# Moving an expert block's transposes into another block's second layer, in a fused attention, MLP and mixture-of-experts kernel

## The chip, the cores and the metric

The kernel runs on one core of one Trainium2 chip. The metric is the device time of one execution in microseconds (us). The engines are named as the profile names them: PE is TensorE (PEld its weight loads), DVE is VectorE, ACT is ScalarE, POOL is GpSimd, SP is SyncE.

## The reference, cut to what matters

Three stages follow each other: attention in chunks of 32 positions, an MLP with a sigmoid gate over the 1536 tokens of 512 numbers that come out of it, and a mixture of 8 experts in which each token goes to the one expert with the largest logit. The change touches the third stage:

```python
logits = x @ w_gate                       # 1536 x 8
expert_idx = np.argmax(logits, axis=1)
gate_w = softmax(logits)[arange(N), expert_idx]
# disp[e]: the tokens of expert e in order, at most cap = 384 of them
h = np.maximum(np.einsum('ecd,edf->ecf', disp, w1), 0.0)   # d = 512, f = 1024
y = np.einsum('ecf,efd->ecd', h, w2)
out[i] = gate_w[i] * y[expert_idx[i], pos[i]]              # for each kept token i
```

## The kernel before

**Precision.** Each product of two float32 matrices is made as three TensorE products: both operands are split into a high part and the rest, and high times high, high times rest and rest times high are summed in PSUM. The expert weights are split on the core: a piece is 128 x 1024 numbers (512 KB), loaded by SyncE's queue into one of eight "raw" tiles (L239), the high part is made on ScalarE (L293) and the rest on VectorE (L298). An expert has eight pieces, four for w1 and four for w2. The split pieces lie in six slots of two pieces. The pieces of an expert are made while the one before it is computed: `w_next(e, keep)` converts the next piece unless `keep` pieces of expert e+1 are done, and a slot must be free. `KEEPS` gives the three bounds of `keep`: after the first layer of an expert, after the second layer of its first block, and in the last part. Inside the first layer, `PUMPS` and `PUMPS1` say behind which group of matmuls a piece is converted.

**Experts and blocks.** The tokens of an expert are handled in blocks of up to 128: first, second and third. The experts are worked in the order `EORDER`; below, "expert 0" is the first of that order. The number of tokens is only known on the chip, so the engines branch on counts read into registers (`tc.If`, `both`): an expert with one block runs `first_of`, one with two `first_of_two` (both blocks in one first layer, 256 columns, L862). Then `thirds_first` branches on a third block: `small_h` where it has at most 64 rows ("narrow": high part and rest lie side by side in one operand), `wide_h` where it has more, `skip` where there is none: one tiny matmul (L1001). After it the two slots of w1 are free. `after_arms` makes the gate and the second layer of the first block (L985), `second` or `second_not` and `rest` the other blocks; a narrow block's output is made by `small2` (L922, then L925 to L928). The If arms are scheduled as a unit; the instructions around them are placed by a list scheduler, which may draw an independent instruction ahead of a branch, and `in_order` keeps a stretch of code in the order written.

**Rows of the tokens.** A block's tokens are gathered from a table in memory by an indirect DMA on GpSimd's queue (L812) into a tile "xr" of a pool with six of them in rotation, transposed on TensorE (L829), and copied by ScalarE (L833) and VectorE (L834) into the split operand "xs". `next_trans` makes the transposes of the next expert's two blocks behind the first layer of an expert (in `first_of`: ahead of the last four transposes, `turn`, of its hidden layer, L954). The finished rows are scattered into the output by an indirect DMA on the same queue (L995, L928).

**The first block.** The first block of expert 0 is computed ahead of the branches, between the steps of the routing of the last tokens (`first_block`): a generator of 50 steps, nearly each one matmul, drawn by `go`. Its second layer (L767) ends the stage. Then the counts are read, expert 0's second block is gathered and transposed (`parts[0].load(1)`, `parts[0].trans(1)`), an arm for fewer than 128 tokens is branched over (L1109), and `first_of(1)` makes that block's first layer (L945).

## Time and profile before

| what | us |
|---|---|
| median of 3 runs | 534.36 |
| lowest, highest run | 533.71, 535.32 |
| the profiled execution, its own time | 533.77 |
| its span, from the first instruction to the last | 531.9 |
| attention, MLP and routing, up to the first matmul of expert 0's second block | 352.5 |
| from there to the end of the span | 179.4 |

The mean TensorE clock that the chip granted was 0.992 of full speed. The page of the profile gives busy times and shares of the span by engine; the views used below list waits by engine and line, instructions in order of time, the chain of work that ended last, and DMA issues with their time to landing. Lines as L945 are lines of the kernel before.

### The profile page before, as it was taken

To read this page: it belongs to the slowest core of one execution; us is meant where nothing else is said; L and a number is where in the kernel's file an instruction comes from. 1 tells how busy PE (TensorE), PEld (TensorE's weight loads), DVE (VectorE), ACT (ScalarE), POOL (GpSimd) and SP (SyncE) were. 2 spreads that over 40 slices of the span, in tenths; PEclk is the share of its full clock that TensorE was granted. 3 is DMA by queue.
4 is the path that set the end of the run, shared out by engine and by line. 5 is a ranking of instruction groups with operands and counts; after the bars stand their busy time and mean duration, and the time that the engine had idled before them with its cause. 6 is when DMAs were issued, how large, how long until landed. Compare 5 with 4: busy or idle time off the path is not lost. (4 is left out here: it accounts for less than half of the span.)

```text
span 531.9 us, 10859 instructions
## 1 busy us (share of the span) xinstructions
PE 509.4 (96%) x4192; PEld 438.5 (82%) x4192; DVE 312.1 (59%) x609; ACT 275.2 (52%) x553; POOL 117.1 (22%) x114
## 2 busy tenths in 40 slices
PE   8799999999999999999999999989999898899994
PEld 3589888898998899989988888768888786789893
DVE  4999894588892282322256444738446757756631
ACT  2798986856752352222255334547355665654521
POOL 3244442332410031000000000252113322311121
PEclk9899999999999999999999999999999999999997
DMA  8888555041440004000059301599536868855010
GB/s 306 277 327 307 199 188 172 1 160 63 171 148 15 0 2 159 0 1 1 10 168 286 110 36 49 168 319 351 195 116 222 282 234 257 290 215 173 23 29 29
DMA packets 38913, 80.62 MB, mean 152 GB/s; under 512 B 3897, under 2 KB 10041, under 8 KB 38842
## 3 DMA queue, kind: packets, MB, share of 16 engines
q1 hardware_dynamic: 36010, 70.66, 39.2%
q0 software_dynamic: 2832, 9.01, 5.2%
q8 instruction: 45, 0.74, 0.6%
q14 instruction: 26, 0.21, 0.1%
HBM read 70.16 MB, written 9.75 MB: 150 GB/s over the span
## 5 line engine op out<-in xcount | busy, mean ns | idle before, releaser
L545 PEld LDWEIGHTS psh<-xT,w 128*128 128x128 f32 x1152 | 147.0, 188 | 8.3 <-DVE xT L518 0.4
L588 PE MATMUL acc<-w,g 128*128 128x512 f32 x576 | 153.0, 400 | 0.0
L545 PE MATMUL psh<-xT,w 128*128 128x256 f32 x1152 | 151.9, 281 | 0.1
L588 PEld LDWEIGHTS acc<-w,g 128*128 128x128 f32 x576 | 100.6, 188 | 19.5 <-issue 2.1
L560 ACT ACTIVATE sg<-psh 128x256 f32<-128x256 f32 x96 | 36.8, 384 | 126.0 <-PE psh L545 124.3
L298 DVE TENSOR_TENSOR w<-raw,w 128x1024 fp32r<-128x1024 f32 x64 | 76.4, 1222 | 30.2 <-ACT w L293 26.6
L568 DVE TENSOR_TENSOR g<-sg,g 128x256 fp32r<-128x256 f32 x78 | 38.2, 490 | 80.3 <-ACT g L564 77.7
L293 ACT ACTIVATE w<-raw 128x1024 fp32r<-128x1024 f32 x64 | 65.4, 1054 | 13.1 <-PE psy L1001 10.0
L862 PE MATMUL psh<-xs,w 128*128 128x256 f32 x480 | 59.2, 283 | 3.8 <-DVE hT L866 3.8
L862 PEld LDWEIGHTS psh<-xs,w 128*128 128x128 f32 x480 | 57.9, 188 | 4.4 <-DVE hT L866 4.2
L985 PE MATMUL psy<-w,hT 128*128 128x512 f32 x240 | 59.8, 401 | 0.0
L985 PEld LDWEIGHTS psy<-w,hT 128*128 128x128 f32 x240 | 44.0, 188 | 9.7
L812 POOL DMA_INDIRECT xr<-rows,taker x21 | 30.1, 1432 | 33.2 <-DVE small L791 15.9
L564 ACT ACTIVATE g<-psh 128x256 fp32r<-128x256 f32 x96 | 36.4, 380 | 0.0
L599 DVE SCALAR_TENSOR_TENSOR x<-acc,x 128x512 f32<-128x512 f32 x36 | 24.1, 686 | 20.1 <-PE acc L588 20.1
L721 POOL DMA_INDIRECT y<-rows,taker x1 | 1.2, 1224 | 123.8 <-DVE cnt_i L728 123.8
L865 ACT ACTIVATE hT<-psh 128x256 fp32r<-128x256 f32 x40 | 14.5, 380 | 25.8 <-PE psh L862 25.8
L866 DVE SCALAR_TENSOR_TENSOR hT<-psh,hT 128x256 fp32r<-128x256 f32 x40 | 16.1, 421 | 19.2 <-ACT hT L865 19.0
L298 POOL TENSOR_TENSOR w<-w,w 128x512 fp32r<-128x512 f32 x12 | 16.7, 1400 | 41.6 <-ACT w L293 41.6
L263 ACT ACTIVATE w<-raw 128x512 f32<-128x512 f32 x32 | 21.3, 676 | 8.4 <-DMA raw<-in_w_out_dram 6.8
L288 POOL TENSOR_TENSOR w<-w,rest 128x512 int32<-128x512 int32 x13 | 17.4, 1340 | 36.8 <-DVE w L274 33.8
L274 DVE SCALAR_TENSOR_TENSOR w<-raw,w 128x512 int32<-128x512 int32 x32 | 24.7, 780 | 0.3
(153 smaller groups left out, 568.0 us busy)
## 6 DMA issues: line engine op xcount, KB each, us to landing
raw<-in_w_dram SPq DMA_DIRECT2D x64, 512.0 KB, 5.7
raw<-in_w_out_dram SPq DMA_DIRECT2D x16, 512.0 KB, 4.4
raw<-in_w_in_dram SPq DMA_DIRECT2D x16, 512.0 KB, 3.7
vt<-in_v_dram SPq DMA_DIRECT2D x12, 512.0 KB, 5.3
kt<-in_k_dram SPq DMA_DIRECT2D x12, 368.0 KB, 5.4
qt<-in_q_dram SPq DMA_DIRECT2D x12, 256.0 KB, 5.0
out_dram<-blank SPq DMA_DIRECT2D x12, 256.0 KB, 2.7
rows<-x SPq DMA_DIRECT2D x5, 520.0 KB, 4.8
```

Source lines behind the costliest of these rows:

```text
L274: nc.vector.scalar_tensor_tensor(out=self.w, in0=self.words()[1], scalar=-0x40000000, in1=self.w, op0=ALU.bitwise_and, op1=ALU.bitwise_or)
L293: nc.scalar.activation(out=w_dst(self.name, self.i, 0), in_=w, func=AF.Copy)
L298: eng.tensor_tensor(out=lo, in0=w, in1=hi.bitcast(F32), op=ALU.subtract)
L545: nc.tensor.matmul(ps, lhsT=w[:, wz, c, i * P:(i + 1) * P], rhs=xT[tb][:, xz, c, :], start=n == 0, stop=n == 3 * KC - 1)
L560: nc.scalar.activation(out=sg_t[u], in_=h_t[u], func=AF.Silu, scale=1.702)
L564: g_last[:1] = [nc.scalar.activation(out=g[:, 0], in_=h_t.pop(u), func=AF.Silu, scale=1.702).ins]
L568: lo = eng.tensor_tensor(out=g[:, 1], in0=sg_t.pop(u), in1=g[:, 0].bitcast(F32), op=ALU.subtract)
L588: nc.tensor.matmul(acc_t[tb][s], lhsT=g[:, gz, s * P:(s + 1) * P], rhs=w[:, wz, wi, :], start=i == 0 and n == 0, stop=u == last_of(k, tb) ...
L599: nc.vector.scalar_tensor_tensor(out=dst, in0=acc_t[tb][s], scalar=1 / 1.702, in1=dst, op0=ALU.mult, op1=ALU.add)
L812: return nc.gpsimd.indirect_dma_start(out=t, out_offset=None, in_=rows[:, :], in_offset=bass.IndirectOffsetOnAxis(ap=taker[:, b, ex:ex + 1 ...
L862: mm = nc.tensor.matmul(ps, lhsT=w[:, wz, c, f0:f0 + P], rhs=t[:, xz, c, :], start=m == 0, stop=m == 3 * KC - 1)
L985: nc.tensor.matmul(ps, lhsT=h[:, hz, fc, o:o + P], rhs=w[:, wz, fc % 4, :], start=fc == 0 and n == 0, stop=fc == F2 - 1 and n == 2)
```

## The change

Five things change together.

1. **The second block of expert 0** is gathered (`load1`) before the rest of the first block's steps, and transposed eight steps before their end (`TAIL1`), into the tile that held the first block's operand, which is not read any more then. `adopt` hands that tile to the expert. The arm that is branched over takes its PSUM tiles from the pool "t" in place of "h".
2. **Room in SBUF:** the operand's tile moves to another pool; the gathered blocks have five tiles "xr" in place of six, and one "xrt" for third blocks in place of two.
3. **The first two chunks of the second layer** (`HEAD2`, six matmuls) move into the arms of the third block (`start2`): behind the transposes where there is one, in place of the tiny matmul where there is none.
4. **Weight pieces** are dealt 3, 4, 1 over the three parts of an expert in place of 3, 2, 3 (`KEEPS`), and the first pump of `first_of` is left out (`PUMPS1`).
5. **Narrow outputs** are scaled by the gate on VectorE, in the two operations that bring the halves together, in place of a third operation on ScalarE.

```diff
--- before.py
+++ after.py
@@ -39,14 +39,16 @@
 AHEAD = 4
 EARLY = 12
 KEEP = 4
-KEEPS = (3, 5, 8)
+KEEPS = (3, 7, 8)
 HALF = P // 2
-PUMPS1 = (1, 1, 1, 0)
+HEAD2 = 2
+PUMPS1 = (0, 1, 1, 0)
 GFC = 2
 EORDER = (1, 2, 0, 3, 4, 5, 6, 7)
 KNOWN = 8
 TFC = 5
 STEPS = (2, 4, 2, 5, 4)
+TAIL1 = 8
 DEPTH = 2
 STOP = False
 U1 = 74
@@ -613,7 +615,9 @@
             nc.tensor.transpose(ps[:, c * P:(c + 1) * P], x2[:, gi, c * P:(c + 1) * P], ident)
         s = gi - gs[0]
         if s == 0:
-            x2T_t[gi] = pool.tile([P, KC, len(gs) * P], F32, tag=f"x2T{len(gs)}", name="x2T", bufs=SUB + 1 - len(gs))
+            width = ROW if len(gs) == 1 else DM * len(gs)
+            t = pool.tile([P, width], F32, tag=f"x2T{len(gs)}", name="x2T", bufs=SUB + 1 - len(gs))
+            x2T_t[gi] = t[:, :DM * len(gs)].rearrange("p (c n) -> p c n", c=KC)
         nc.scalar.activation(out=x2T_t[gs[0]][:, :, s * P:(s + 1) * P], in_=ps.rearrange("p (c n) -> p c n", n=P),
                              func=AF.Copy)
 
@@ -710,7 +714,7 @@
         def load():
 
             f = first_block
-            f.xs = late_t["pool1"].tile([P, 2, KC, P], F32R, name="xs0")
+            f.xs = late_t["xs"]
             f.h = late_t["pool1"].tile([P, 2, F2, P], F32R, name="hT0")
             f.xr = late_t["y0"]
             nc.vector.tensor_scalar(out=taker0, in0=tk_t[0][:, EORDER[0]:EORDER[0] + 1], scalar1=float(NT), scalar2=None,
@@ -727,11 +731,19 @@
             nc.tensor.matmul(ps[:, :E], lhsT=ones, rhs=ohacc[:, 0], start=True, stop=True)
             nc.vector.tensor_copy(cnt_i[:, E:], ps[0:1, EORDER[0]:EORDER[0] + 1])
 
-        def trans():
+        def load1():
+            late_t["x1"] = late_t["pool"].tile([P, ROW], F32, tag="x2T1", name="x1", bufs=SUB)
+            return nc.gpsimd.indirect_dma_start(
+                out=late_t["x1"], out_offset=None, in_=rows[:, :],
+                in_offset=bass.IndirectOffsetOnAxis(ap=taker[:, 1, EORDER[0]:EORDER[0] + 1], axis=0),
+                bounds_check=NT, oob_is_err=False).ins
+
+        def trans(xr=None):
             f = first_block
             ps = psum("misc", "pst0")
+            xr = f.xr if xr is None else xr
             for c in range(KC):
-                nc.tensor.transpose(ps[:, c * P:(c + 1) * P], f.xr[:, c * P:(c + 1) * P], ident)
+                nc.tensor.transpose(ps[:, c * P:(c + 1) * P], xr[:, c * P:(c + 1) * P], ident)
             pv = ps.rearrange("p (c n) -> p c n", n=P)
             nc.scalar.activation(out=f.xs[:, 0], in_=pv, func=AF.Copy)
             nc.vector.tensor_tensor(out=f.xs[:, 1], in0=pv, in1=f.xs[:, 0].bitcast(F32), op=ALU.subtract)
@@ -741,7 +753,7 @@
             f = first_block
             order = [(xz, wz, c) for xz, wz in ((0, 0), (0, 1), (1, 0)) for c in range(KC)]
             p1 = [psum("lg", "psh0"), psum("acc0", "psh1")]
-            t = late_t["pool"].tile([P, KC, SUB * P], F32, tag=f"x2T{SUB}", name="hs0", bufs=1).rearrange("p c n -> p (c n)")
+            t = late_t["pool"].tile([P, SUB * DM], F32, tag=f"x2T{SUB}", name="hs0", bufs=1)
             f.hs = [t[:, 512 * j:512 * j + 512] for j in range(2)]
 
             def first(j, i):
@@ -804,10 +816,13 @@
     def expert_parts(e, ep, tp, cnt):
 
         ex = EORDER[e]
-        xr, xs, gt, hT = {}, {}, {}, {}
+        xr, xs, gt, hT, own = {}, {}, {}, {}, {}
+
+        def adopt(b, x):
+            own[b] = x
 
         def load(b):
-            t = ep.tile([P, ROW], F32, tag="xr" if b < 2 else "xrt", name="xr", bufs=6 if b < 2 else 2)
+            t = ep.tile([P, ROW], F32, tag="xr" if b < 2 else "xrt", name="xr", bufs=5 if b < 2 else 1)
             xr[b] = t
             return nc.gpsimd.indirect_dma_start(
                 out=t, out_offset=None, in_=rows[:, :],
@@ -816,6 +831,8 @@
 
         def xs_of(b):
 
+            if b in own:
+                return own[b], 0
             i = min(b, 2)
             key = 0 if i < 2 else b
             if key not in xs:
@@ -870,7 +887,7 @@
         def block(b):
 
             with in_order():
-                block_h(b)()
+                block_h(b, kind="t")()
                 layer2_part(b, y_of(b), range(F2))
             send(b)
 
@@ -890,6 +907,7 @@
                 pv = ps[:, :KC * HALF].rearrange("p (c n) -> p c n", n=HALF)
                 nc.scalar.activation(out=x[:, :, 0], in_=pv, func=AF.Copy)
                 nc.vector.tensor_tensor(out=x[:, :, 1], in0=pv, in1=x[:, :, 0].bitcast(F32), op=ALU.subtract)
+                start2()
                 hs = []
                 for j in range(2):
                     w_tile(("w1", e, j), 0)
@@ -922,14 +940,13 @@
                     nc.tensor.matmul(ps, lhsT=h[:, fc].rearrange("p z n -> p (z n)"), rhs=w[:, wz, fc % 4, :],
                                      start=fc == 0 and wz == 0, stop=fc == F2 - 1 and wz == 1)
             y = ep.tile([P, DM], F32, tag="y", name="y", bufs=2)[:HALF]
-            nc.vector.tensor_copy(y, ps[HALF:])
-            nc.vector.tensor_tensor(out=y, in0=ps[:HALF], in1=y, op=ALU.add)
-            nc.scalar.activation(out=y, in_=y, func=AF.Copy, scale=gt[b][:HALF])
+            nc.vector.tensor_scalar(out=y, in0=ps[HALF:], scalar1=gt[b][:HALF], scalar2=None, op0=ALU.mult)
+            nc.vector.scalar_tensor_tensor(out=y, in0=ps[:HALF], scalar=gt[b][:HALF], in1=y, op0=ALU.mult, op1=ALU.add)
             nc.gpsimd.indirect_dma_start(
                 out=out[:, :], out_offset=bass.IndirectOffsetOnAxis(ap=taker[:HALF, b, ex:ex + 1], axis=0),
                 in_=y, in_offset=None, bounds_check=NT - 1, oob_is_err=False)
 
-        def block_h(b, pump=lambda i: None):
+        def block_h(b, pump=lambda i: None, kind="h"):
 
             x, o = xs_of(b)
             h = hT_of(b)
@@ -939,7 +956,7 @@
                 w_tile(("w1", e, j), 0)
                 w = w_tile(("w1", e, j), 1)
                 if j not in p1:
-                    p1[j] = psum("h", "psh")
+                    p1[j] = psum(kind, "psh")
                 for xz, wz in ((0, 0), (0, 1), (1, 0)):
                     for c in cs:
                         nc.tensor.matmul(p1[j], lhsT=x[:, xz, c, o:o + P], rhs=w[:, wz, c, :],
@@ -949,7 +966,7 @@
                     nc.scalar.activation(out=hs[j], in_=p1[j], func=AF.Relu)
 
             def turn(j):
-                ps = psum("h", "psu")
+                ps = psum(kind, "psu")
                 for c in range(KC):
                     nc.tensor.transpose(ps[:, c * P:(c + 1) * P], hs[j][:, c * P:(c + 1) * P], ident)
                 n0 = b * P if b < 2 else 0
@@ -986,7 +1003,7 @@
                                      start=fc == 0 and n == 0, stop=fc == F2 - 1 and n == 2)
 
         def layer2(b):
-            layer2_part(b, y_of(b), range(F2))
+            layer2_part(b, y_of(b), range(HEAD2 if b == (1 if e == 0 else 0) else 0, F2))
             send(b)
 
         def send(b):
@@ -1054,10 +1071,18 @@
 
         def wide_h(b):
             trans(b)
+            start2()
             block_h(b)()
 
+        def start2():
+
+            b = 1 if e == 0 else 0
+            layer2_part(b, y_of(b), range(HEAD2))
+
         def thirds_first():
 
+            y_of(1 if e == 0 else 0)
+            assert NCB == 3
             for b in range(2, NCB):
                 hT_of(b)
                 xs_of(b)
@@ -1065,8 +1090,7 @@
                 def first():
                     both(cnt[ex] > b * P + HALF, lambda: wide_h(b), lambda: small_h(b))
 
-                y_of(1)
-                both(cnt[ex] > b * P, first, lambda: skip(1))
+                both(cnt[ex] > b * P, first, start2)
             for j in range(F // 512):
                 w_free(("w1", e, j))
 
@@ -1131,7 +1155,7 @@
             y_of(1)
             both(cnt[ex] > P, second, second_not)
 
-        return SimpleNamespace(load=load, trans=trans, xs_of=xs_of, after_first=after_first, others=others,
+        return SimpleNamespace(adopt=adopt, load=load, trans=trans, xs_of=xs_of, after_first=after_first, others=others,
                                before_arms=before_arms)
 
 
@@ -1176,6 +1200,7 @@
             wp2 = ctx.enter_context(tc.tile_pool(name="wp2", bufs=1, side="left"))
             free_slots.append(wp2.tile([P, 2, 2048], F32R, name="w4"))
             late_t["y0"] = wp2.tile([P, ROW], F32, name="y0")
+            late_t["xs"] = wp2.tile([P, 2, KC, P], F32R, name="xs0")
             late_t["known"] = wp2.tile([P, NCB * E], F32, name="known")
             plg = st.enter_context(tc.tile_pool(name="ps_lg", bufs=1, space=PSUM))
             ps_pools["lg"] = (plg, "lg", [P, 512])
@@ -1317,6 +1342,9 @@
             first_block.gate()
             while (("w2", 0, 1), 1) not in ready:
                 w_pump()
+            not_before.append(first_block.load1())
+            go(33 - TAIL1)
+            first_block.trans(late_t["x1"])
             go()
             first_block.finish()
     rt.close()
@@ -1337,13 +1365,11 @@
         free_slots.append(wp3.tile([P, 2, 2048], F32R, name="w5"))
         late_raw(RAWS)
         parts = [expert_parts(e, ep, tp, cnt) for e in range(E)]
-        not_before.append(parts[0].load(1))
-        with ExitStack() as behind:
-            for i in parts[0].trans(1):
-                behind.enter_context(tc.issue_after(i))
-            w_loads(8)
-            while w_next(-1):
-                pass
+        parts[0].load(1)
+        parts[0].adopt(1, late_t["xs"])
+        w_loads(8)
+        while w_next(-1):
+            pass
         w_end[0] = len(pieces)
         with tc.high_priority(offset=LOADS):
             w_loads(8 * (F // 512))
```

## Rows read from the trace of the kernel before

**Rows 1.** The page, busy time and share of the span by engine.
```profile
PE 509.4 (96%) x4192; PEld 438.5 (82%) x4192; DVE 312.1 (59%) x609; ACT 275.2 (52%) x553; POOL 117.1 (22%) x114
```

**Rows 2.** TensorE's waits from 350 us: waiter, releaser, total us, times, longest.
```profile
PE psh L862 <- DVE hT L866: 3.8, 2, 1.9
PE psu L954 <- ACT hs L949: 1.9, 1, 1.9
PE psh L945 <- ACTq L1109: 1.7, 1, 1.7
PE psh L900 <- DVE xs L892: 1.0, 1, 1.0
```

**Rows 3.** Timeline of the last narrow output: start, us, instruction, idle time before it.
```profile
524.49 0.69 DVE L925 COPY y<-psy 64x512 f32<-64x512 f32 x1 [2.49 <-DMA out_dram<-y,taker]
525.22 0.68 DVE L926 TENSOR_TENSOR y<-psy,y 64x512 f32<-64x512 f32 x1
525.98 0.72 ACT L927 ACTIVATE y<-y,gt 64x512 f32<-64x512 f32 x1 [4.37 <-issue]
```

**Rows 4.** TensorE's timeline, from the first block to expert 0's second.
```profile
350.11 0.60 PE L829 MATMUL pst<-ident,xr 128*128 128x128 f32 x4
...
352.52 4.48 PE L945 MATMUL psh<-w,xs 128*128 128x512 f32 x18 [1.71 <-ACTq L1109]
```

**Rows 5.** TensorE's timeline at expert 1's third block.
```profile
378.51 4.22 PE L985 MATMUL psy<-w,hT 128*128 128x512 f32 x17
382.66 0.46 PE L889 MATMUL pst<-ident,xr 64*128 64x64 f32 x4
384.10 4.00 PE L900 MATMUL psh<-w,xs 128*128 128x512 f32 x16 [0.98 <-DVE xs L892]
```

**Rows 6.** Tile xs, 340 to 390 us: ns min/median/max, first and last start.
```profile
L833 ACT ACTIVATE xs<-pst x5: 588/592/603, 350.9 to 378.8; 128x512 fp32r<-128x512 f32 x5
```

**Rows 7.** VectorE's timeline at expert 1's third block.
```profile
378.98 1.29 DVE L834 TENSOR_TENSOR xs<-pst,xs 128x512 fp32r<-128x512 f32 x2 [0.23 <-ACT xs L833]
...
380.61 1.23 DVE L298 TENSOR_TENSOR w<-raw,w 128x1024 fp32r<-128x1024 f32 x1
383.62 0.42 DVE L892 TENSOR_TENSOR xs<-pst,xs 128x256 fp32r<-128x256 f32 x1 [1.79 <-ACT xs L891]
```

**Rows 8.** GpSimd's timeline from 340 us, its gathers and scatters.
```profile
342.76 1.83 POOL L812 DMA_INDIRECT xr<-rows,taker  x1 [15.94 <-DVE small L791]
...
379.90 1.02 POOL L812 DMA_INDIRECT xr<-rows,taker  x1 [0.36 <-ACT ex L839]
...
404.06 0.93 POOL L928 DMA_INDIRECT out_dram<-y,taker  x1 [4.76 <-DMA out_dram<-y,taker]
405.30 1.16 POOL L812 DMA_INDIRECT xr<-rows,taker  x1 [0.30 <-POOLq L1047]
```

**Rows 9.** DMA issues from 404 to 407 us: median us from issue to landing.
```profile
xr<-rows,taker POOLq DMA_INDIRECT x1, 4.9
```

**Rows 10.** The chain that ended last, in expert 2: start, us, what.
```profile
407.05 0.87 PE pst L829 x8
...
412.46 0.11 PE psy L1001
```

**Rows 11.** Timelines of ScalarE, VectorE and TensorE between experts 4 and 5.
```profile
452.69 1.06 ACT L293 ACTIVATE w<-raw 128x1024 fp32r<-128x1024 f32 x1 [2.25 <-PE psy L1001]
...
453.78 1.22 DVE L298 TENSOR_TENSOR w<-raw,w 128x1024 fp32r<-128x1024 f32 x1 [1.65 <-ACT w L293]
456.30 5.77 DVE L298 TENSOR_TENSOR w<-raw,w 128x1024 fp32r<-128x1024 f32 x5 [1.29 <-PE psh L862]
...
454.53 6.01 PE L862 MATMUL psh<-xs,w 128*128 128x256 f32 x48
```

**Rows 12.** ScalarE's timeline at the start of expert 4.
```profile
442.85 0.72 ACT L927 ACTIVATE y<-y,gt 64x512 f32<-64x512 f32 x1 [3.86 <-issue]
...
444.42 0.58 ACT L949 ACTIVATE hs<-psh 128x512 f32<-128x512 f32 x1
```

**Rows 13.** The branches of one line on TensorE: ns min/median/max, first and last start.
```profile
L1047 PEldq COMPARE_BRANCH  x45: 65/184/3665, 359.6 to 520.0; - x45
```

## The prediction

> **What bounds the kernel now.** I read the page first: TensorE is busy 96% of the span, VectorE 59%, ScalarE 52% [rows 1]. So TensorE's order of work sets the end, and an edit counts only if it takes work off TensorE, fills one of its holes, opens a new one, or shortens what comes after its last matmul. The view of who waited for whom, cut to TensorE in the expert phase (from 350 us), names the holes [rows 2]: two of 1.9 us in the first layer of the two-block experts (L862 behind VectorE's L866), one of 1.9 us in L954 behind ScalarE's L949, one of 1.7 us where the first expert's second block starts (L945, behind ScalarE's queue at the branch L1109), one of 1.0 us in the narrow third block (L900). Together 8.4 us. The reader is to see that all five are waits for ScalarE or VectorE, none for weights from memory. Behind the last matmul follow a copy, an addition and a scaling before the last rows go out [rows 3].
>
> The arms taken can be read from the timeline: in the order of work, experts 0 to 7, only expert 1 has a third block (narrow), experts 2 and 4 have one block, 3, 6 and 7 a narrow second one.
>
> **Part 1, the early transposes.** Before, the four transposes L829 run when the first block is done, and the next matmul starts at 352.52 after 1.71 us of idling [rows 4]. The wait is put down to ScalarE reaching the branch L1109: the untaken arm shares the PSUM tiles "h" with L945. The change moves the arm to the tiles "t" and makes the transposes eight steps before the end. A step is 0.24 us (17 matmuls L985 start 4.15 us before the next group, [rows 5]), so eight cover 1.95 us; copy and subtraction take 0.59 us and 0.65 us [rows 6, 7], 1.3 us with the handoffs. The gather that feeds them is issued where the first one is now, at 342.76 [rows 8], more than 5 us ahead of them, and another gather follows it on GpSimd's queue, which shifts those behind it by 1.3 us. The weight loads on SP's queue are held for this gather as they now are for the first, so they start as before. TensorE does the same work; the hole goes: -1.7 us. Bounds: 0 (the start still waits for something ScalarE does at the branch) and -1.7. I take the full gain, since both causes that I can see are removed. If the cover were gone, it would cost 1.3 us.
>
> **Part 2, buffers.** To make room, the gathered blocks "xr" get five tiles in place of six, in rotation. Asked for in program order they are: expert 0's second block (#0), expert 1's two (#1, #2), expert 0's first, in the untaken arm (#3), expert 2's (#4, #5), expert 3's (#6, #7), and so on. With six, #7 reuses #1 and #8 reuses #2. The trace agrees: one gather is issued at 379.90, behind expert 1's first gate (L839), the next at 405.30, behind that expert's second arm and its last scatter at 404.06, which itself waits for the scatter before it [rows 8]. With five, #6 reuses #1 (so 379.90) and **#7, expert 3's second block, reuses #2**, so it goes to 405.30. It lands 4.9 us later [rows 9], at 410.2. But expert 2 has one block and is short: it makes expert 3's transposes from 407.05 on, eight in 0.87 us [rows 10], the second four at 407.5. So TensorE would stand for 2.7 us, in a place where it never waits now. All that stands in the order behind them (L954, the second layer) waits too. Bounds: 0 and 4. The other reuses fall at least 10 us ahead of need; the third blocks' single tile is released before its gather's turn on the queue. Cost: +2.7 us.
>
> **Part 3, two chunks of the second layer into the arms.** Six matmuls of the second layer stand in for the dummy L1001 in the arms not taken: seven dummies of 0.11 us go [rows 10], -0.8 us. The scheduler has so far pulled 17 matmuls of the second layer ahead of the third-block branch [rows 5]; they accumulate in one PSUM bank, so now none can pass the six. Where the arm is empty, TensorE does them later at no loss. Where it is taken (expert 1) it loses cover: from the start of the 17 to L900 were 5.59 us [rows 5]. Now VectorE has L834 twice to 380.27, a weight piece from 380.61 to 381.84, and L892 of 0.42 us [rows 7], so L900 can start at 382.30, 3.79 us after the same point; 11 matmuls fewer (2.68 us) lie in it, so idling grows by 2.68 - 1.80 = 0.9 us. Bounds: -0.7 (piece not ahead of it) and +0.9. I take +0.9: the piece is ahead today.
>
> **Part 4, pieces 3, 4, 1, the first pump gone, scaling on VectorE.** Weight pieces from the fifth on need a slot that comes free when TensorE has passed the third-block arm: today ScalarE idles 2.25 us for L1001 (expert 4) and VectorE 1.65 us, and then five pieces in one row (5.77 us) keep VectorE from L866, with the first layer's 48 matmuls of 6.01 us done and waiting [rows 11]. With the 17 matmuls behind the arm, the slot comes about 2.7 us sooner, and three pieces run under the second layer, not one. Work it out from the end of the twelve matmuls that make hs, in expert 4: VectorE's line is hs and one piece on ScalarE (0.58 + 1.06), ten pieces of 1.15, four subtractions of 0.65 to 0.7, gate 0.3, L866 0.4: 16.6 us; TensorE until it needs the bank back: 36 matmuls of 0.24, 16 transposes of 0.11, dummy 0.1, 48 of 0.122: 16.4 us. 0.2 us is left of the hole of 1.9. I take -1.6 us, as that assumes VectorE never idles (bounds 0 and -1.9). The same hole after expert 2 goes for certain if part 2 holds TensorE up by 2.7 us there: -1.9.
>
> The hole at L954: L949 starts at 444.42, because L927 of the narrow output before it sits in ScalarE's queue until 442.85, and the pump's piece follows [rows 12]. Both leave the queue, and L949 then waits for its own twelve matmuls alone, with six more queued ahead of L954 (1.4 us, against 0.58 for L949); -1.9 us, bounds 0 and -1.9. Behind L927 now nothing is queued on ScalarE; VectorE's two operations stay two, each with a PSUM operand as before, so 0.7 us each by [rows 3].
>
> At the end, the scaling of 0.72 us and its handoff of 0.08 go [rows 3]: -0.8 us.
>
> **Sum**, against the profiled execution's own 533.77 us (span 531.95 and 1.8 around it; 0.6 us under the median of the runs): -1.7 + 2.7 - 0.8 + 0.9 - 1.6 - 1.9 - 1.9 - 0.8 = -5.1, so **528.6 us**.
>
> **Rivals.**
> (a) *The gather is in time.* If the tiles aren't reused as I count, or the landing is hidden, the 2.7 us don't come, and the hole after expert 2 shrinks like the other (-1.6, not -1.9): 533.8 - 7.5 = 526.2 us. For it: I have the rotation only from the order of issues. Against: the two issues behind expert 1's gates fit it.
> (b) *The transition gains nothing.* L945 also depends on what ScalarE does last in the first block, or on the branch through another tile: 528.6 + 1.7 = 530.3 us.
> (c) *Slower: code behind the branch.* TensorE's branches take 0.18 us in the median, but up to 3.67 us [rows 13]. Today 17 matmuls (4.1 us) stand queued ahead of the third-block branch and hide that; afterwards eight transposes of 0.87 us, so a long one would show 2.8 us. Three of the seven arms where it struck would give 528.6 + 8.4 = 537 us, and it takes three for a slower kernel. Against: today's long branches lie at the narrow second arms, and TensorE's queue is already past the branch 2 us before the matmuls end. The Trainium skill ("Runtime: NRT & Kernel Launch", section Instruction fetch mechanics) says that a taken branch to a target outside the loaded pages forces a fetch by DMA before the engine goes on, and the duplicated matmuls make the arms longer; by that rule each such jump costs, while by the row most of 45 cost nothing to be seen.
>
> **How the numbers follow.** My forecast 0.57, (a) 0.20, (b) 0.14, (c) 0.06, something unseen 0.03. A difference of 0.3% (1.6 us) is about what a measurement of this kernel can tell. The range takes in (a) less 0.4 and the forecast with (b), and the bounds of part 2 (4 us of standing) with no gain at the first layer: 525.8 to 531.8 us. Faster by over 0.3% needs all the gains of 3.5 us to survive: the forecast, (a) and most of (b), 0.85. Within 0.3%: a part of (b) with the bounds against it, 0.08; slower: (c) and half of the unseen, 0.07.
>
> **What would show it.** Part 1: L945 follows L1001 of the transition at once. Part 2: TensorE waits in L829 for a gather by L812 in expert 2, some 2.7 us, and that gather is issued just behind a scatter L928 or its line afterwards. Part 3: seven fewer L1001; the wait of L900's line grows to nearly 2 us. Part 4: no wait of L954's line for L949, and less than 1 us of L862's for L866. End: no ScalarE instruction between the narrow output's two on VectorE and the last scatter. The forecast is wrong if TensorE waits behind the arms' branches, or not at all in expert 2.

## The result, and the profile after

The changed kernel takes 526.5 us (median of four runs, 525.63 to 527.21), the kernel before 534.84 in the runs made beside it: ratio 0.9846, 95% interval 0.9821 to 0.9872, so 1.3% to 1.8% faster. The prediction was 528.6, from 525.8 to 531.8; the time that came is near that of its rival (a), 526.2. The profiled execution of the changed kernel has 525.63 us of its own and a span of 523.8, which is 8.1 us less than before.

The five holes of [rows 2] first. TensorE's waits in the same stretch of the changed kernel (waiter, releaser, total us, times, longest):

```profile
PE pst L906 <- DVE xs L851: 1.2, 1, 1.2
PE psh L962 <- ACT y L806: 0.8, 1, 0.8
PE psy L1002 <- ACT xs L850: 0.7, 1, 0.7
PE psh L962 <- issue: 0.6, 1, 0.6
PE psh L918 <- DVE xs L909: 0.3, 1, 0.3
PE psh L879 <- DVE hT L883: 0.2, 1, 0.2
```

The lines have moved: the first layer L862 is L879 here, the second L985 is L1002, the block's first layer L945 is L962, the turn L954 is L971, the dummy L1001 is L1018, the narrow block's L889 and L900 are L906 and L918. Of 8.4 us in the large holes 3.8 us are left. The two behind the first layer and the one at the turn are gone but for 0.2; the one where the first expert's second block starts is half its size and has another releaser; the narrow third block's has grown from 1.0 to 1.2 + 0.3 (L906 and L918); and two are new, 0.7 ahead of L1002 and 0.6 ahead of L962.

Where the time came from shows when the expert phase is cut where each expert's first layer starts, from the end of the first block on. TensorE's windows of the kernel before (window, its length, busy time and matmuls, granted clock, DMA share, GB/s; experts 0, 1, 3, 4 and 5, and what follows the last matmul):

```profile
350.71:366.19 15.48, 13.77 (x68) 1.00 1.03 364
366.19:400.85 34.66, 33.68 (x206) 1.00 0.60 196
...
414.44:438.74 24.30, 22.39 (x146) 1.00 0.76 260
438.74:454.53 15.79, 13.85 (x68) 1.00 0.80 251
454.53:480.90 26.37, 24.45 (x155) 1.00 0.74 255
...
524.40:531.90 7.50, 0.00 (x0) 0.63 0.08 17
```

And of the changed kernel:

```profile
349.48:364.22 14.74, 13.91 (x68) 1.00 1.03 377
364.22:399.49 35.27, 33.82 (x205) 1.00 0.63 221
...
412.90:435.82 22.92, 22.10 (x145) 1.00 0.93 316
435.82:449.40 13.58, 13.54 (x65) 1.00 0.69 240
449.40:474.31 24.91, 24.10 (x155) 1.00 0.95 321
...
516.92:523.80 6.88, 0.00 (x0) 0.67 0.09 19
```

Stage by stage the difference is -0.74, +0.61, -0.18, -1.38, -2.21, -1.46, -0.49, -0.40 and -0.62: -6.87 us in all, with the granted clock at 1.00 in all eight expert stages of both. The other 1.2 us of the 8.1 lie ahead of the first stage: its start moved from 350.71 to 349.48, with expert 0's four early transposes ahead of it in both. That point falls between 348.3 and 351.9 in the profiled executions of all kernels of this study, so 1.2 us there can't be told from scatter. Experiments are therefore read below by the time from this point to the end of the span: 181.2 before, 174.3 after.

**Where there is no wait.** The prediction's dearest term was a stand of 2.7 us in expert 2, for expert 3's second gather. TensorE's timeline there, in the changed kernel (start, us, instruction; idle time before it in brackets):

```profile
405.51 1.04 PE L846 MATMUL pst<-ident,xr 128*128 128x128 f32 x8
406.46 0.66 PE L971 MATMUL psu<-ident,hs 128*128 128x128 f32 x4
407.08 5.78 PE L1002 MATMUL psy<-w,hT 128*128 128x512 f32 x24
```

All eight transposes stand in one group with no idle time. GpSimd's timeline has the gathers at the same two places as [rows 8]:

```profile
377.95 1.02 POOL L827 DMA_INDIRECT xr<-rows,taker  x1 [0.37 <-ACT ex L856]
...
403.98 0.93 POOL L945 DMA_INDIRECT out_dram<-y,taker  x1 [4.94 <-DMA out_dram<-y,taker]
405.21 1.15 POOL L827 DMA_INDIRECT xr<-rows,taker  x1 [0.30 <-ACT hT L975]
```

The gather at 405.21 is issued while the transposes run, and they don't wait for it: expert 3's second block was already there, from 377.95. (That gather is the ninth of L827; in the run with four tiles below, the ninth is the one that TensorE waits for.)

**The transition.** TensorE's timeline, against [rows 4]:

```profile
347.39 2.09 PE L779 MATMUL psy<-w,hT 128*128 128x512 f32 x8
350.26 3.06 PE L962 MATMUL psh<-w,xs 128*128 128x512 f32 x12 [0.78 <-ACT y L806]
```

The transposes are out of the way and the branch is no longer named. What is left, 0.78 us, is a wait for the copy of the first block's output (L806).

**The end**, against [rows 3]:

```profile
517.01 0.75 DVE L943 TENSOR_SCALAR y<-psy,gt 64x512 f32<-64x512 f32 x1 [2.48 <-DMA out_dram<-y,taker]
517.80 0.74 DVE L944 SCALAR_TENSOR_TENSOR y<-psy,gt,y 64x512 f32<-64x512 f32 x1
518.82 0.91 POOL L945 DMA_INDIRECT out_dram<-y,taker  x1 [3.56 <-DVE y L944]
```

The scaling on ScalarE is gone; the two operations on VectorE take 0.75 and 0.74 us, where the copy and the addition took 0.69 and 0.68.

### The profile page after: what moved, and what is told of

Its sections match the earlier page's. It is cut to its first block, busy times and chain, and to the rows that moved or that the text cites. A ratio compares the mean times of both kernels' runs of the same rounds, so it can differ in the third digit from the quotient of the medians.

```text
span 523.8 us, 10850 instructions
## 1 busy us (share of the span) xinstructions
PE 507.5 (97%) x4185; PEld 437.7 (84%) x4185; DVE 312.1 (60%) x609; ACT 273.5 (52%) x549; POOL 119.5 (23%) x115
## 4 chain that ended last, share of the span: by engine, by line
PE 86%; DVE 3%; ACT 3%; issue 3%; DMA 2%; POOL 1%; another core or an unknown queue 0%; SPq 0%; POOLq 0%; DVEq 0%; ACTq 0%
PE acc L590 25%; PE psh L547 25%; PE psy L1002 9%; PE psh L879 9%; PE psh L962 3%; PE pse L505 2%; PE psy L940 2%; PE pss L435 1%; DVE w L300 1%; DMA kt<-in_k_dram 1%; PE psy L779 1%; PE pst L846 1%; PE psr L615 1%; PE psh L763 1%; ACT w L295 1%
## 5 line engine op out<-in xcount | busy, mean ns | idle before, releaser
L879 PE MATMUL psh<-xs,w 128*128 128x256 f32 x480 | 58.8, 283 | 0.3 <-DVE hT L883 0.2
L1002 PE MATMUL psy<-w,hT 128*128 128x512 f32 x240 | 57.8, 397 | 0.8 <-ACT xs L850 0.7
L879 PEld LDWEIGHTS psh<-xs,w 128*128 128x128 f32 x480 | 57.6, 189 | 0.9 <-DVE hT L883 0.7
L1002 PEld LDWEIGHTS psy<-w,hT 128*128 128x128 f32 x240 | 44.5, 188 | 11.3 <-issue 1.6
L827 POOL DMA_INDIRECT xr<-rows,taker x21 | 29.2, 1391 | 17.8 <-ACTq L1064 10.0
L883 DVE SCALAR_TENSOR_TENSOR hT<-psh,hT 128x256 fp32r<-128x256 f32 x40 | 16.2, 420 | 21.1 <-ACT hT L882 21.0
L295 ACT ACTIVATE w<-w 128x512 fp32r<-128x512 f32 x32 | 19.8, 628 | 9.8 <-POOL w L290 5.0
```

Of the source, the lines that this page charges most:

```text
L295: nc.scalar.activation(out=w_dst(self.name, self.i, 0), in_=w, func=AF.Copy)
L827: return nc.gpsimd.indirect_dma_start(out=t, out_offset=None, in_=rows[:, :], in_offset=bass.IndirectOffsetOnAxis(ap=taker[:, b, ex:ex + 1 ...
L879: mm = nc.tensor.matmul(ps, lhsT=w[:, wz, c, f0:f0 + P], rhs=t[:, xz, c, :], start=m == 0, stop=m == 3 * KC - 1)
L1002: nc.tensor.matmul(ps, lhsT=h[:, hz, fc, o:o + P], rhs=w[:, wz, fc % 4, :], start=fc == 0 and n == 0, stop=fc == F2 - 1 and n == 2)
```

## The experiments

All of the computation is done in every experiment. Ratios are to the kernel before, timed beside the experiment on the same chip; its median there is 535.86 to 537.07 us, not 534.84, so times in us of different experiments aren't compared with each other without it.

**The weight pieces' hole: slots or dealing?** Two runs, each undoing one of the two edits that could have closed the hole behind L879. In the first the pieces are dealt as before:

```
-KEEPS = (3, 7, 8)
+KEEPS = (3, 5, 8)
```

> The changed kernel with the weight pieces dealt 3, 2, 3 again, all else changed. Slot theory: the two holes of 1.9 us in the first layer went because the slots of w1 come free 2.7 us sooner; then they stay away (under 0.6 us in all) and the time stays within 1 us of 526.5. Deal theory: they went because three pieces no longer follow in one row at the end of an expert; then 1 to 1.9 us come back at each of two places, 528.5 to 530.

Ratio 0.9902 [0.9856, 0.9949], 529.4 us, 178.4 from the first stage to the end. TensorE's waits, and VectorE's timeline ahead of the first of the two:

```profile
PE psh L879 <- DVE hT L883: 4.0, 2, 2.0
```

```profile
414.56 5.77 DVE L300 TENSOR_TENSOR w<-raw,w 128x1024 fp32r<-128x1024 f32 x5 [1.61 <-PE psh L879]
```

Both holes are back at full size, with five pieces in one row ahead of L883 as in [rows 11]. The early slot alone does nothing for them.

In the second run part 3 is undone, so that the slot comes late again, with the new dealing left:

```
-HEAD2 = 2
+HEAD2 = 0
...
-            b = 1 if e == 0 else 0
-            layer2_part(b, y_of(b), range(HEAD2))
+            pass
...
-                both(cnt[ex] > b * P, first, start2)
+                both(cnt[ex] > b * P, first, lambda: skip(1))
```

> The changed kernel without the six matmuls in the arms (the tiny matmul is back, and the second layer can be drawn ahead of the branch again). Slot theory: the slots come late again, both holes of the first layer return (1 to 1.9 us each), the dummies cost 0.8 us, and the narrow third block's wait falls from 1.5 to 1.0 us: 529 to 531. Deal theory: no holes, only dummies and the third block: near 526.8. Code theory (branches on TensorE that take long are seen since the 17 matmuls no longer cover them): the 0.6 and 0.7 us seen at the branches go, 525.5 to 529.

Ratio 1.0045 [1.0019, 1.0071], 538.3 us. TensorE's waits, and the first of the two in its timeline:

```profile
PE psh L879 <- DVE hT L883: 5.6, 2, 4.3
PE psh L879 <- ACTq L1064: 1.5, 2, 0.7
PE psh L879 <- issue: 1.3, 1, 1.3
```

```profile
422.72 8.06 PE L879 MATMUL psh<-xs,w 128*128 128x256 f32 x48 [4.28 <-DVE hT L883]
```

VectorE's row of pieces ahead of it, and TensorE's window behind it:

```profile
416.57 5.77 DVE L300 TENSOR_TENSOR w<-raw,w 128x1024 fp32r<-128x1024 f32 x5 [1.67 <-ACT w L295]
```

```profile
422.72:427.45 4.73, 4.73 (x22) 0.50 1.01 327
```

The dealing alone is worse than neither, 8.4 us of waits at L879 against 3.8. So neither theory holds by itself: both edits (0.2), neither (3.8, the kernel before), slot alone (4.0), dealing alone (8.4). In the changed kernel six pieces run in a row from 448.16 on, 1.24 us ahead of the first layer's first matmul (449.40), where the five of [rows 11] start 1.77 us behind it; 0.27 us of idling stand ahead of them where [rows 11] have 1.65 and 1.29. VectorE's timeline between experts 4 and 5:

```profile
448.16 6.91 DVE L300 TENSOR_TENSOR w<-raw,w 128x1024 fp32r<-128x1024 f32 x6 [0.27 <-DVEq L1064]
```

With the dealing alone the row of five starts later still, 4.08 us behind the first layer's first matmul (412.49), where the run with the slot alone has 1.78 (414.56 against 412.78); why it starts later isn't settled by these runs.

**A stand can cost more than its length.** Behind the 4.28 us TensorE's granted clock is 0.50 for 4.7 us, the lower of its two levels (1.2 GHz, not 2.4), and the 48 matmuls of L879 take 8.06 us where the changed kernel takes 5.96. So 2.1 us come on top of the standing. In the run with the slot alone the clock falls behind one of the two stands (1.97 us; the 48 matmuls take 7.51) and not behind the other (1.98 us; 5.97), and in the kernel before it stays at 1.00 behind all of its holes, of up to 1.94 us. The length of a stand alone therefore doesn't tell whether the clock falls behind it.

**The turn's hole: scaling or pump?** One run puts the scaling back on ScalarE, the other the first pump:

```
-            nc.vector.tensor_scalar(out=y, in0=ps[HALF:], scalar1=gt[b][:HALF], scalar2=None, op0=ALU.mult)
-            nc.vector.scalar_tensor_tensor(out=y, in0=ps[:HALF], scalar=gt[b][:HALF], in1=y, op0=ALU.mult, op1=ALU.add)
+            nc.vector.tensor_copy(y, ps[HALF:])
+            nc.vector.tensor_tensor(out=y, in0=ps[:HALF], in1=y, op=ALU.add)
+            nc.scalar.activation(out=y, in_=y, func=AF.Copy, scale=gt[b][:HALF])
```

> The changed kernel with the narrow outputs scaled on ScalarE again. The end grows by 0.7 to 0.8 us. At expert 4's start, if the scaling's place in ScalarE's queue made the hole of 1.9 us together with the pump's piece (my theory), about 0.9 us of it come back (the piece of 1.05 is still gone): 528.1. If the pump's piece alone made it, none: 527.2.

```
-PUMPS1 = (0, 1, 1, 0)
+PUMPS1 = (1, 1, 1, 0)
```

> The changed kernel with the first pump of a one-block first layer back. My theory: without the scaling in its queue ScalarE stands idle some 5 us before expert 4's first hs, so the piece runs there and makes no hole: 526.5 within 0.6. Rival: the piece sits ahead of hs and holds TensorE up by up to 1 us at the experts with one block, 527.5 to 528.5.

With the scaling back: 527.36 us, ratio 0.9856 [0.9813, 0.9899]. The profiled execution is the slowest of five, 531.47, with 177.8 us from the first stage to the end: TensorE stands 1.76 us in expert 0 ahead of the second layer, and its 24 matmuls behind that take 7.40 us, not 5.86, with the clock at 0.50. The end is 0.74 us longer (7.62 from the last matmul, against 6.88). But expert 4 takes 13.59 us as in the changed kernel (13.58); ScalarE's timeline there (L966 is one line further down):

```profile
442.54 0.72 ACT L945 ACTIVATE y<-y,gt 64x512 f32<-64x512 f32 x1 [3.47 <-issue]
444.47 0.60 ACT L967 ACTIVATE hs<-psh 128x512 f32<-128x512 f32 x1 [1.21 <-PE psh L963]
```

The scaling is there, is done at 443.26, and ScalarE then idles for TensorE: the hole that I expected from it does not come. With the pump back: 525.01 us, ratio 0.9827 [0.9774, 0.988], 174.6 from the first stage to the end, expert 4 in 13.57. So the hole stays closed with either of the two edits undone, and the scaling shows its worth at the end alone. A run with both undone wasn't made, so that one of the two closes the hole isn't shown, and the rows speak for a third cause. In [rows 12] the scaling starts 4.11 us after expert 4's first matmul (442.85 against 438.74); here, back on ScalarE, it starts 1.23 us after it (442.54 against 441.31), because VectorE's copy ahead of it starts 0.27 us before that matmul, not 2.62 us behind it. A piece of 1.05 us behind it would end at some 3.0 us (an estimate from these rows), ahead of the 3.16 at which the copy L967 starts.

**The gather's tiles.** One tile fewer, to see whether the wait that I had forecast exists at all:

```
-            t = ep.tile([P, ROW], F32, tag="xr" if b < 2 else "xrt", name="xr", bufs=5 if b < 2 else 1)
+            t = ep.tile([P, ROW], F32, tag="xr" if b < 2 else "xrt", name="xr", bufs=4 if b < 2 else 1)
```

> The changed kernel with four tiles for gathered blocks in place of five. Theory of release order (a new block takes the tile that was released first, the untaken arm's among them): expert 3's second block now takes the tile of expert 1's second, its gather moves from 378 to about 405, and TensorE waits 3 to 4.5 us in the transposes of expert 2: 529.5 to 531. Theory of strict rotation, as in the prediction: expert 2's second block would take the tile of expert 1's first and be gathered only behind expert 1's gate, so a wait of over 5 us stands in expert 1 instead. Theory of hidden landing: no wait in either, 526.5.

535.83 us, ratio 0.9978 [0.994, 1.0015], 185.0 from the first stage to the end: nearly all of the gain is gone. TensorE's timeline in experts 2 and 4:

```profile
404.98 0.60 PE L846 MATMUL pst<-ident,xr 128*128 128x128 f32 x4
409.53 1.11 PE L846 MATMUL pst<-ident,xr 128*128 128x128 f32 x4 [3.95 <-DMA xr<-rows,taker]
...
451.09 1.12 PE L846 MATMUL pst<-ident,xr 128*128 128x128 f32 x4 [4.31 <-DMA xr<-rows,taker]
```

The first four transposes have their rows, the second four stand 3.95 us; GpSimd's timeline has the gather that they wait for where part 2 had put it, behind the last scatter of expert 1:

```profile
402.63 0.92 POOL L945 DMA_INDIRECT out_dram<-y,taker  x1 [2.92 <-DMA out_dram<-y,taker]
403.86 1.98 POOL L827 DMA_INDIRECT xr<-rows,taker  x1 [0.30 <-PE psu L971]
```

So the mechanism of part 2 is real, and needs four tiles, not five. Expert 4 has the same wait, which I had not foreseen. The two stands are 8.3 of the 10.7 us that this stretch is longer than in the changed kernel; the clock is at 0.50 behind both, and TensorE's busy time in it is 166.8 us against 163.5. That the untaken arm's block keeps no tile explains it; whether tiles go out by order of release or in a rotation that leaves this block out isn't told apart, since both give these rows.

**What is left at the transition.** L806 reads the bank of the first block's output, and L962 waits for it. Two runs: one swaps that bank with one of the first layer's, the other puts the output into the pool "misc", whose banks go to the second layers' tiles afterwards and not to those of L962 (by the order in which the pools are opened).

```
-            p1 = [psum("lg", "psh0"), psum("acc0", "psh1")]
+            p1 = [psum("lg", "psh0"), psum("acc1", "psh1")]
...
-            f.ps = psum("acc1", "psy0")
+            f.ps = psum("acc0", "psy0")
```

> The changed kernel with the PSUM banks of the first block's second hidden half and of its output exchanged. If the 0.8 us before expert 0's second block is a wait for the bank that the first block's output is read from, it goes: 525.7, and the matmul follows at once. If it is a wait for ScalarE's place in its queue or for the operand, it stays: 526.5.

```
-            f.ps = psum("acc1", "psy0")
+            f.ps = psum("misc", "psy0")
```

> The changed kernel with the first block's output summed in a PSUM bank that afterwards belongs to the pool of the second layers, not to that of the hidden halves. If the 0.8 us before expert 0's second block is a wait for the whole old pool in whose place the new one lies (exchanging its two banks changed nothing), it goes: the matmul follows at once, -0.8 us. If the matmul waits for the operand or for ScalarE's order, the 0.8 us stay.

The swap changes nothing: 526.13 us, ratio 0.9783 [0.9737, 0.9829], 174.3 from the first stage to the end, and TensorE's waits have the same line still, `PE psh L962 <- ACT y L806: 0.8, 1, 0.8`. With the other pool it is gone (525.27 us, ratio 0.9784 [0.9735, 0.9832], 173.0 from the first stage to the end); TensorE's timeline:

```profile
348.37 2.11 PE L779 MATMUL psy<-w,hT 128*128 128x512 f32 x8
350.31 3.89 PE L962 MATMUL psh<-w,xs 128*128 128x512 f32 x16
```

So the wait is not one bank's: it stays with either bank of that pool, and goes with another pool. That the new tiles wait for the last reader of the whole old pool explains both; no other account was tested.

**The narrow third block.** Half of the chunks that expert 1's arm carries go ahead of the narrow transposes, with two chunks more in the arms:

```
-HEAD2 = 2
+HEAD2 = 4
...
+                start2(range(0, 2))
...
-                start2()
+                start2(range(2, HEAD2))
...
-        def start2():
+        def start2(fcs=range(HEAD2)):
...
-            layer2_part(b, y_of(b), range(HEAD2))
+            layer2_part(b, y_of(b), fcs)
```

> The changed kernel with four chunks of the second layer in the arms, in the narrow third block two ahead of its transposes and two behind. If the 1.2 us at the transposes is a wait for the PSUM tile that the next expert's transposes are read from, and the 0.3 us behind them is the copies, both go (-1.2 to -1.5 us at expert 1): 525.2. If the longer arms make TensorE's branches cost more, that eats it: 526.5 or more.

526.65 us, ratio 0.9796 [0.9749, 0.9843]. The waits ahead of L906 and L918 are gone and expert 1 takes 33.89 us, not 35.27. But expert 3 takes 26.03, not 22.92. TensorE's timeline there, and its branches from 418 to 436 us (ns min/median/max, first and last start):

```profile
423.51 1.04 PE L846 MATMUL pst<-ident,xr 128*128 128x128 f32 x8
426.59 3.92 PE L1003 MATMUL psy<-w,hT 128*128 128x512 f32 x10 [2.05 <-ACTq L1065]
```

```profile
L1065 PEldq COMPARE_BRANCH  x6: 70/198/3745, 422.3 to 433.6; - x6
```

One branch of 3.7 us ahead of the arm, and TensorE stands 2.05 us behind it: rival (c)'s picture. The clock falls to 0.50 behind this stand, and the second layer's 24 matmuls take 7.38 us, not the 5.82 of the changed kernel. The same with the swapped banks:

> Both of the last two edits together. If the two holes are independent: -2.0 to -2.3 us against the changed kernel, 524.3. If one only moves the other: 525.2 to 526.

527.78 us, ratio 0.9804 [0.9746, 0.9863]; 2.4 us at the same place and 1.7 at a second one, in expert 0, with L806's 0.8 as it was.

**Code or work?** The changed kernel already has branches that show. Its own, over the expert phase, from 430 to 436 us and from 456 to 464 us:

```profile
L1064 PEldq COMPARE_BRANCH  x43: 65/190/4550, 357.6 to 512.6; - x43
...
L1064 PEldq COMPARE_BRANCH  x3: 181/318/4550, 430.0 to 431.1; - x3
...
L1064 PEldq COMPARE_BRANCH  x2: 187/1284/2380, 460.1 to 460.3; - x2
```

The one of 4.55 us begins at 431.1, and L962 stands 0.62 us to 435.82. The one of 2.38 us, in the last row, ends at 462.7, and L1002 stands 0.70 us to 463.00. If such branches come from where the code lies, instructions that never run must move them. Two runs put 32 and 64 dummies (64 and 128 instructions, each with its weight load) into an arm that is taken by no expert:

```
+                for _ in range(32):
+                    skip(0)
```

> The changed kernel with 32 tiny matmuls (64 instructions) in the arm that is never taken, ahead of all experts: no work is added, only the code behind it lies further back. Code theory (TensorE's long branches depend on where the code lies): the branches of over 2 us stand at other places, and the visible standing behind branches (1.3 us in the changed kernel) comes out otherwise, anywhere from 0 to 4 us. Semaphore theory (they are waits for other engines): the same branches are long at the same places, and the waits stay within 0.3 us.

> As the run before, with 64 tiny matmuls (128 instructions) in the untaken arm. Code theory: other places again, 0 to 4 us visible. Semaphore theory: the same places and waits.

No work is added, and with 32 the time goes to 528.8 us (ratio 0.9856 [0.981, 0.9902]; 178.4 from the first stage to the end, 4.1 more), with 64 to 525.79 (0.9795 [0.9748, 0.9842]; 175.6). With 32, a wait in expert 0, TensorE's timeline in expert 3, its window there and its branches:

```profile
PE psy L1002 <- issue: 1.5, 1, 1.5
```

```profile
429.32 5.04 PE L1002 MATMUL psy<-w,hT 128*128 128x512 f32 x14 [2.58 <-ACTq L1064]
```

```profile
429.80:433.21 3.41, 3.41 (x9) 0.50 0.78 235
```

```profile
L1064 PEldq COMPARE_BRANCH  x2: 187/2226/4265, 424.5 to 424.8; - x2
```

The long branch now sits ahead of the arm, 4.3 us, and shows 2.58; in the timeline neither L962 in expert 4 nor L1002 in expert 5 waits any more, where the changed kernel had its 0.6 and 0.7, so the wait put down to L850 came from the code as well. Of the 4.1 us some 2.8 are standing (2.58 and 1.53 in place of 0.62 and 0.70) and some 1.5 the clock, at 0.50 behind the 2.58: the 24 matmuls take 7.37 us in place of 5.82. With 64 dummies there are two, 1.3 us in expert 0 and 1.1 ahead of that L962.

What a long branch waits for is in the traces' DMA packets: the queue that loads instructions (q8) moves one packet of 16 KB while that branch of 4.3 us lasts:

```profile
q8 instruction: 1, 0.02, 1.6%
```

In the fourteen profiled executions TensorE has 56 branches of over 1 us from 340 us on, and each of them ends 1.3 to 1.5 us after such a packet has landed. So a long branch is one that waits for its instructions; where the code lies decides which branch that is, and what TensorE has queued ahead of it decides what shows. Code that isn't moved scatters too: the wait ahead of expert 0's second layer is 0 in the changed kernel, 0.2 us with four gather tiles and 0.6 with the banks swapped.

**Both finds together**: the split, the other pool and 64 dummies in the untaken arm.

> The changed kernel with the two edits that each took a wait away (four chunks in the arms, two of them ahead of the narrow third block's transposes; the first block's output in the other PSUM bank) and 64 tiny matmuls in the untaken arm, which only move the code. Without more standing behind branches than the changed kernel has (1.3 us): -0.7 and -1.4 us, 524.4 against its 526.5. If the long branch falls on expert 3's third-block branch, as it did in both kernels with the longer arms alone, 2 to 3 us come back there: 526.5 to 527.

525.95 us, ratio 0.9814 [0.9779, 0.9848]; its profiled execution, the fastest of six, has 172.75 us from the first stage to the end, 1.6 less than the changed kernel, but the interval overlaps that of the changed kernel, so by times it is not shown to be faster.

## Why the prediction was right, and where it was not

The direction and the size were right, 526.5 in a range of 525.8 to 531.8; the likeliest case was not. One step failed outright, and three terms had the wrong size.

**The failed step is part 2's "in rotation":** that with five tiles "#7, expert 3's second block, reuses #2". It cost 2.7 us in the sum and 0 on the chip. The order of issues that I took as proof fits another count as well, in which the block of expert 0's untaken arm holds no tile; with four tiles the wait comes, 3.95 us. I had rival (a) for this, at 0.20. The price was too low as well: where a stand of 2.58 us did come (32 dummies), the clock fell behind it and cost some 1.5 us more.

**Part 1** was sized -1.7 and gave -0.93. The wait at the branch went, and one for the reader of an old PSUM tile came out behind it, 0.78 us; that is the half of rival (b) which said that L962 also depends on what ScalarE does last in the first block.

**Part 3's dummies** were sized by the 0.11 us of the chain [rows 10], -0.8 in all, and gave more. Before, 24 matmuls of the second layer with a dummy among them took 5.99 us in expert 3 (L985 to L922) and 6.01 in expert 6; without it 5.66 and 5.67 (L1002 to L940), so 0.33 to 0.34 each, some 2.0 us over the arms that aren't taken in experts 2 to 7, less about 0.2 given back in each of experts 2 and 4. The row to read was that of the weight loads in the kernel before, which idle 0.33 us ahead of each dummy:

```profile
PEld L1001 <- issue: 4.0, 12, 0.4
```

Its other half, the cover lost at the narrow third block, was sized +0.9; idling grew by 0.47 (0.98 to 1.17 + 0.28) and the stage by 0.61. VectorE did what I had counted: the narrow block's subtraction L909 starts at 379.80, right behind a weight piece, and L918 (380.27) starts 3.70 us after the point that I counted from, 0.80 us behind the start of the eight transposes (375.77), where I had 3.79. What was off is the price of the 11 matmuls that moved out: 2.50 us (42 take 9.84 where 31 took 7.34), not 2.68. With both, 2.50 - (5.59 - 3.70) = 0.61. The place was off too: most of the idling, 1.17 us, stands ahead of the narrow transposes, for L851, and not behind them.

**Part 4** held: -1.92 after expert 4 (forecast -1.6), -1.94 at the turn (-1.9), -0.62 at the end (-0.8, the two operations on VectorE being 0.06 us dearer each). After expert 2 -1.71 came for the right size (-1.9) by the wrong reason: no stand in expert 2 gave VectorE time. And at the turn the credit that I shared between two edits isn't shown to belong to either: the hole stays closed without the one or the other, and VectorE's earlier pieces may have closed it.

**Rival (c)** was 0 in the sum and came true in small: +1.3 us, 0.6 and 0.7 behind long branches, each of which ends 1.5 us after a packet of instructions has landed. The Trainium skill ("Runtime: NRT & Kernel Launch", section Instruction fetch mechanics) has a taken branch wait for a fetch when its target lies outside the loaded pages. The traces agree, with a 16 KB packet at each of the 56 long branches, and most of the 43 here take 0.2 us; the page gives no time for one.

Together: -0.9 - 2.0 + 0.4 + 0.5 - 1.9 - 1.7 - 1.9 - 0.6 + 1.3 = -6.8, against -6.87 by stages. The forecast of -5.1 was near by luck: the wait that never came (+2.7) was partly paid for by the branches (1.3) and by the half hole of part 1 (0.8). That rival (a)'s 526.2 was met so closely is luck too: its -7.5 is more than the stages gave, and the 1.2 us ahead of them, which no term stood for, made up the rest.

## What to carry to other kernels

Who reuses whose buffer is worth counting from a run with one buffer fewer, not from the order of issues, which fits more than one count. A hole with one releaser can have a second right behind it, so a moved producer should be credited only down to the next one in line. With branches in the program, the position of the code is worth up to 4 us here, so a gain of that size should be read by stages, and the matmuls queued ahead of a branch kept as its cover. A forecast stand of TensorE should carry a second price, that of the matmuls behind it at the lower clock, 1.5 to 2.1 us for one stand here.

## What the runs showed of the hardware that was not expected

- The same work with 32 or 64 unrun dummies more took 178.4 and 175.6 us from the first stage to the end, against 174.3 with none: branches of TensorE of 2 to 4.6 us move from place to place, while the median one takes 0.19. Each of the 56 over 1 us ends 1.3 to 1.5 us after a 16 KB packet of instructions has landed.
- The granted clock fell to 0.50 behind single stands of 1.8 to 4.3 us, and 24 matmuls of the second layer then took 7.4 us, not 5.8; behind others of 1.9 to 2.0 us it stayed at 1.00.
- A dummy matmul that appears for 0.11 us in the chain costs 0.33 to 0.34 us among the second layer's matmuls.
- Scaling in an operation that reads PSUM on VectorE (64x512) took 0.75 and 0.74 us where the copy and the addition without it took 0.69 and 0.68.
